# An FFT filter with a soft mixture of experts on one core: another pace for the third chain, two small units two slots later, one copy on ScalarE

## The chip, the cores and the metric

One core of a Trainium2 chip. Its engines are called by the profile's names: PE is TensorE (PEld its weight loads), DVE is VectorE, ACT is ScalarE, POOL is GpSimd, SP is SyncE, which issues nearly all transfers here. The metric is the device time of one execution in microseconds, the median of several runs.

## What is computed

```python
def _attn_ref(x, filt_r, filt_i):            # x: 8 batches, 2496 rows, 256 columns
    X = np.fft.rfft(x, axis=1)
    y = np.fft.irfft(X * (filt_r + 1j * filt_i)[None], n=x.shape[1], axis=1)
...
def _moe_ref(x, phi, w1, w2):                # x: 19968 x 256; 8 experts, 4 slots each
    logits = x @ phi
    d = softmax of logits over the 19968 rows;  slot_input = d.T @ x
    per expert: slot_out = relu(slot_input @ w1) @ w2
    c = softmax of logits over the 32 slots;    return c @ slot_out
```

The filtered sequence is the input of the second part. The first softmax runs over all rows, so it is kept as a running maximum and sum while batch after batch is filtered.

## The kernel before

The length 2496 is split as 39 x 64. Batches 1 to 7 go through these steps, and the steps of neighbouring batches overlap.

- **Units.** A batch's x comes in six pieces, called units 0 to 5 (`PIECE`). `fold_x` (L336, L339) adds and subtracts the two halves of a unit into a tile `eo`, on POOL from batch 2 on; there are two `eo` buffers, so a fold starts when the unit before the last one has been read. `s1_unit` (L357) multiplies a unit on PE into a PSUM tile of a pool with one buffer, ScalarE copies it to `at` (L366), and SP writes `at` to `a_dram`. Unit 0 is half as large as the others.
- **Slots.** Each batch has ten slots. Slot n = 10 b + c loads a tile `ash` from `a_dram`; `x_unit` (L435) multiplies it on PE, DVE makes the two products with the filter (L455, L457) and the two adds that give `yt` (L458, L459; the adds go to POOL for batches 6 and 7). Two slots later `t_unit` (L467) transposes `yt` on PE, ScalarE copies it to `y` (L481), and after every second one `l_unit` (L494) makes logits, copied to `lt` (L505).
- **Which unit in which slot.** `slot_of` gives each unit (b, u) a slot; `split_next` does the fold one slot ahead, and with it the load of a later piece of x.
- **Chains.** When a group of batches is through (0 and 1; 2 and 3; 4 and 5; 6; 7), a chain of dependent work begins (`chain`, L543 on): logits back to the time domain (`ltr`, `v1`, `v`, `lg`), their maximum (`cm`, `cmax`, then `mt`, `mx`, `mb`, `m_run`), the exponentials `d` (L634 on DVE, L635 on ScalarE), a transform of these (`u`, `u2`, `dd`), their sum `z`, and the weighted sum `s` of the rows `y`. Its small tiles use a PSUM pool of two buffers. The chain is a generator: each `yield` is a mark, and after each slot `hop_slot` lets it go some marks further, two (`HOPS`), or for the third chain as many as `PACE` says, slot by slot. So the marks and the pace set which slot work lies between two steps of a chain.
- **The end.** When the third chain's last products are done, the buffers that they free take the experts' weights; the last two chains run in a fixed order (`TAIL`); then come the experts (L1048 to L1077) and the outputs (L1104, L1109), 4-byte floats of 19968 x 256.

Within this, a scheduler places the instructions of each engine in one fixed order, from priorities and its own estimate of times; on the chip each engine works its queue off in that order and waits where an input or a buffer is missing.

Below, an instruction is named as the program names its output: s1_4_5 is unit 5 of batch 4, x_3_4 slot 4 of batch 3, u_0_4 a piece of u of chain 0 (the first chain).

## Time and profile before

| | |
|---|---|
| median of 3 runs | 375.63 us (375.1 to 376.7) |
| the profiled execution | 375.31 us, its span 373.5 us |
| PE busy | 344.2 us (92%) |
| DVE busy | 264.6 us (71%) |
| ACT busy | 175.2 us (47%) |
| POOL busy | 147.0 us (39%) |
| moved by DMA | 104.17 MB, mean 279 GB/s |
| mean granted clock of PE | 0.962 |

Times in the rows count from the start of the span. A row of the timeline has the start, the time from the first to the last of the merged instructions, the engine and line, the tiles written and read, how many instructions there are, and in brackets how long the engine had been idle before and what ended the wait. What ended it is inferred from semaphores: where a wait is for several things, the last by the profile is named. An fp32 matrix product is two instructions in the trace and one in the program.

### The profile page before, as it was taken

What the parts mean: (1) busy time and instruction counts of PE and PEld (TensorE: products, weight loads), DVE (VectorE), ACT (ScalarE), POOL (GpSimd) and SP (SyncE); (2) the same over time, 40 slices, a digit from 0 to 9 for tenths busy, and PEclk for the clock granted to TensorE, in tenths of its full rate; (3) what the DMA queues carried; (4) which work ended last, traced back from release to release, by engine and by line L of the source; (5) the groups of instructions that cost most, each with busy time, mean ns of one, the idle gap of its engine ahead of it and who ended that gap; (6) DMA issues with size and microseconds to landing.
All of it is one profiled execution on the core that took longest, in us unless ns stands there. A gap on an engine that the chain in (4) does not pass through costs nothing. (4 is left out here: it accounts for less than half of the span.)

```text
span 373.5 us, 10516 instructions
## 1 busy us (share of the span) xinstructions
PE 344.2 (92%) x4254; PEld 255.9 (69%) x4254; DVE 264.6 (71%) x522; ACT 175.2 (47%) x354; POOL 147.0 (39%) x177
## 2 busy tenths in 40 slices
PE   8999999899998899999889998899989999999950
PEld 6866766677776577867666775777866635878850
DVE  1586897778998969689996847695675552887540
ACT  3466554454555444545625453533354430766430
POOL 0188655545546213724830754332631302650000
PEclk9999999999999999999999999999999999999555
DMA  8999899799799459979853747642898993699996
GB/s 300 395 396 371 291 329 355 233 342 374 222 350 335 143 163 301 314 235 292 307 185 80 224 138 215 255 142 58 299 355 280 326 272 83 253 411 413 417 419 287
DMA packets 50438, 104.17 MB, mean 279 GB/s; under 512 B 5250, under 2 KB 23810, under 8 KB 48214
## 3 DMA queue, kind: packets, MB, share of 16 engines
q1 hardware_dynamic: 49700, 103.16, 79.4%
q8 instruction: 33, 0.54, 0.6%
q10 hardware_dynamic: 690, 0.35, 0.3%
q14 instruction: 15, 0.12, 0.1%
HBM read 63.37 MB, written 40.12 MB: 277 GB/s over the span
## 5 line engine op out<-in xcount | busy, mean ns | idle before, releaser
L435 PE MATMUL x<-cst_t,ash 128*128 128x128 f32 x640 | 85.7, 276 | 1.7 <-DMA ash<-a_dram 1.7
L455 DVE TENSOR_TENSOR t<-x,ff_t 128x512 f32<-128x512 f32 x80 | 55.1, 689 | 39.0 <-PE x L435 30.5
L336 POOL TENSOR_TENSOR eo<-xt 128x512 f32<-128x512 f32 (+1 forms) x37 | 45.2, 1220 | 94.4 <-issue 89.8
L435 PEld LDWEIGHTS x<-cst_t,ash 128*128 128x128 f32 x640 | 78.1, 192 | 4.0 <-DMA ash<-a_dram 2.6
L366 ACT COPY at<-s 128x1024 f32<-128x1024 f32 (+1 forms) x42 | 39.6, 942 | 47.8 <-PE s L357 27.8
L467 PE MATMUL t<-cst_t,yt 128*128 128x128 f32 x320 | 49.9, 278 | 0.0
L339 POOL TENSOR_TENSOR eo<-xt 128x512 f32<-128x512 f32 (+1 forms) x40 | 48.9, 1221 | 0.0
L481 ACT COPY y<-t 128x512 f32<-128x512 f32 x58 | 33.8, 587 | 30.8 <-PE t L467 30.5
L357 PE MATMUL s<-eo,w1q_t 64*64 64x512 f32 (+1 forms) x336 | 42.8, 579 | 2.7 <-POOL eo L339 2.5
L467 PEld LDWEIGHTS t<-cst_t,yt 128*128 128x128 f32 x320 | 35.9, 141 | 10.2 <-issue 7.1
L457 DVE TENSOR_TENSOR x<-x,ff_t 128x512 f32<-128x512 f32 x60 | 41.7, 696 | 1.3
L1104 PE MATMUL out<-so,st 32*128 32x256 f32 x468 | 35.1, 337 | 2.4 <-ACT ob L1109 1.3
L1104 PEld LDWEIGHTS out<-so,st 32*128 32x128 f32 x468 | 30.7, 222 | 6.1 <-ACT ob L1109 2.9
L494 PEld LDWEIGHTS l<-yt,phi_t 128*32 128x32 f32 x640 | 15.2, 109 | 25.5 <-issue 21.1
L1109 DVE COPY ob<-out 128x512 f32<-128x512 f32 (+1 forms) x40 | 25.0, 669 | 8.5 <-DMA out<-ob 5.8
L458 POOL TENSOR_TENSOR yt<-yt,t 128x256 f32<-128x256 f32 x20 | 15.1, 754 | 35.0 <-DVE yt L457 25.4
L1109 ACT COPY ob<-out 128x512 f32<-128x512 f32 (+1 forms) x40 | 21.7, 582 | 14.8 <-DMA out<-ob 7.8
L458 DVE TENSOR_TENSOR yt<-x,t 128x256 f32<-128x256 f32 x60 | 25.2, 420 | 1.3
L494 PE MATMUL l<-yt,phi_t 128*32 128x128 f32 x640 | 25.7, 278 | 0.0
L459 DVE TENSOR_TENSOR yt<-x,t 128x256 f32<-128x256 f32 x60 | 24.8, 413 | 0.0
L528 PE MATMUL s<-y,dd 128*32 128x256 f32 x232 | 19.2, 381 | 0.3 <-ACT dd L682 0.3
L528 PE MATMUL u<-cst_t,d 117*64 117x60 f32 (+3 forms) x440 | 15.2, 221 | 1.2 <-ACT d L635 1.2
(117 smaller groups left out, 482.1 us busy)
## 6 DMA issues: line engine op xcount, KB each, us to landing
xt<-in_x SPq DMA_DIRECT2D x35, 512.0 KB
ash<-a_dram SPq DMA_DIRECT2D x70, 256.0 KB
out<-ob SPq DMA_DIRECT2D x17, 1024.0 KB
a_dram<-at SPq DMA_DIRECT2D x56, 240.0 KB
w<-in_wx SPq DMA_DIRECT2D x33, 256.0 KB
w<-in_wx SPq DMA_DIRECT2D x6, 512.0 KB
x_t<-in_x SPq DMA_DIRECT2D x5, 512.0 KB
ff_t<-in_ff SPq DMA_DIRECT2D x10, 256.0 KB
```

The costliest lines, as they stand in the source:

```text
L336: ins = (dve if (1, 2) < (b, u) < (2, 0) else eng).tensor_tensor(out=eo[:, 0, 0:n], in0=xs[:, :, 0], in1=xs[:, :, 1], op=ALU.add)
L339: ins = eng.tensor_tensor(out=eo[:, 1, 0:n], in0=xs[:, :, 0], in1=xs[:, :, 1], op=ALU.subtract)
L357: ins = pe.matmul(ps, w1q_t[q, c], eo[q, c, 0:n], start=True, stop=True)
L366: act.copy(at[:, 0:n], both[:, :, 0:n].rearrange("q r u d -> q u r d"))
L435: ins = pe.matmul(ps[:, 2 * k + dh].rearrange("q r c -> q (r c)"), ash[:, k, dh * P : (dh + 1) * P], C("a1" if t0 + k else "b0"), start=Tr ...
L455: dve.tensor_tensor(out=t2, in0=ps[:, :, ::-1, :], in1=fiv, op=ALU.mult)
L457: dve.tensor_tensor(out=part, in0=ps, in1=frv, op=ALU.mult)
L458: add.tensor_tensor(out=yt[:, :, 1, :], in0=part[:, :, 1, :], in1=t2[:, :, 1, :], op=ALU.add)
L467: ins = pe.transpose(pt[:, k, dh, :], yt[:, c % 2, 2 * k + dh].rearrange("q r c -> q (r c)"), ident)
L494: ins = pe.matmul(pl[32 * j : 32 * j + 32, :], phi_t[:, dh, :], yt[:, j // 2, 2 * (j % 2) + dh].rearrange("q r c -> q (r c)"), start=(dh = ...
L1104: nc.tensor.matmul(prs[k][:, mm, :], sts[n][q, hs, c0 : c0 + P], so[q, ho], start=(i == 0), stop=(i == 2))
L1109: copy(ob[:, nm * k : nm * (k + 1), :], prs[k])
```

## The change

Three edits: `PACE` has other numbers and the third chain gets one mark more (`lg8`, between the last piece of lg and `mt`), so that its 14 numbers now add up to 24 instead of 23; unit 0 of batches 5 and 7 has slot 10 b - 14 instead of 10 b - 16, that is 36 instead of 34 and 56 instead of 54; the first of the three copies of u2 in the first two chains is ScalarE's instead of DVE's.

```diff
-PACE = (1, 1, 3, 2, 1, 1, 1, 2, 2, 2, 2, 2, 2, 1)
+PACE = (2, 3, 2, 1, 1, 1, 1, 1, 2, 2, 2, 2, 2, 2)
...
-    return CPB * b - 5 - (2 * (NU - 1 - u) if u else CPB + (b > 2))
+    return CPB * b - 5 - (2 * (NU - 1 - u) if u else CPB + (1, -1)[b in (5, 7)] * (b > 2))
...
-        if late:
+        if g >= NG - 3:
             yield "lg8"
...
-            ended[1] = dve.tensor_copy(u2[:, t0 : t0 + n].rearrange("k t h b e -> k t (h b e)"), pu[:, 0:n])
+            copy = act.copy if t0 == 0 and g < NG - 3 else dve.tensor_copy
+            ended[1] = copy(u2[:, t0 : t0 + n].rearrange("k t h b e -> k t (h b e)"), pu[:, 0:n])
```

What it makes of the order is shown at three places. The number at a name's end is the tile's own; lines after 674 are one higher in the changed kernel. On POOL the folds stand in the order (4,4), (5,0), (4,5), (5,1) before and (4,4), (4,5), (5,0), (5,1) in the change, and in the same way for batches 6 and 7.

First place, PE in slots 34 to 36, with the first chain's u; before:

```order
L357 MATMUL s1_5_0_1721<-eo5_0_1653,w1q_t_72 64x256 x4
L467 MATMUL t_3_3_1736<-cst_t_73,yt_3_2_1633 128x128 x4
L435 MATMUL x_3_5_1743<-cst_t_73,ash3_5_1422 128x128 x4
L528 MATMUL u_0_0_1315<-cst_t_73,d_0_1282 64x60 x12
L357 MATMUL s1_4_5_1753<-eo4_5_1697,w1q_t_72 64x512 x4
L494 MATMUL l_3_1_1760<-yt_3_2_1633,phi_t_74 32x128 x8
L528 MATMUL u_0_0_1315<-cst_t_73,d_0_1282 64x60 x4
L528 MATMUL u_0_4_1336<-cst_t_73,d_0_1282 64x60 x16
L467 MATMUL t_3_4_1779<-cst_t_73,yt_3_4_1715 128x128 x4
L435 MATMUL x_3_6_1786<-cst_t_73,ash3_6_1459 128x128 x4
```

In the change, from slot 35 on:

```order
L467 MATMUL t_3_3_1726<-cst_t_73,yt_3_2_1633 128x128 x4
L435 MATMUL x_3_5_1733<-cst_t_73,ash3_5_1422 128x128 x4
L357 MATMUL s1_4_5_1743<-eo4_5_1692,w1q_t_72 64x512 x4
L494 MATMUL l_3_1_1750<-yt_3_2_1633,phi_t_74 32x128 x8
L528 MATMUL u_0_0_1315<-cst_t_73,d_0_1282 64x60 x16
L528 MATMUL u_0_4_1336<-cst_t_73,d_0_1282 64x60 x16
L467 MATMUL t_3_4_1769<-cst_t_73,yt_3_4_1710 128x128 x4
L435 MATMUL x_3_6_1776<-cst_t_73,ash3_6_1459 128x128 x3
L528 MATMUL u_0_8_1389<-cst_t_73,d_0_1282 64x60 x10
L528 MATMUL u_0_8_1389<-cst_t_73,d_0_1282 64x20 x2
L435 MATMUL x_3_6_1776<-cst_t_73,ash3_6_1459 128x128
L357 MATMUL s1_5_0_1788<-eo5_0_1723,w1q_t_72 64x256 x4
```

The small unit s1_5_0 moves from ahead of t_3_3 to behind x_3_6, and s1_4_5 moves ahead of the chain's u.

DVE at the same place, behind the three subtractions d_0; before:

```order
L455 TENSOR_TENSOR t2_3_4_1714<-x_3_4_1709,ff_t_101 128x512
L457 TENSOR_TENSOR x_3_4_1709<-x_3_4_1709,ff_t_101 128x512
L455 TENSOR_TENSOR t2_3_5_1748<-x_3_5_1743,ff_t_101 128x512
L458 TENSOR_TENSOR yt_3_4_1715<-x_3_4_1709,t2_3_4_1714 128x4x64
L459 TENSOR_TENSOR yt_3_4_1715<-x_3_4_1709,t2_3_4_1714 128x4x64
L457 TENSOR_TENSOR x_3_5_1743<-x_3_5_1743,ff_t_101 128x512
L458 TENSOR_TENSOR yt_3_4_1715<-x_3_5_1743,t2_3_5_1748 128x4x64
L459 TENSOR_TENSOR yt_3_4_1715<-x_3_5_1743,t2_3_5_1748 128x4x64
```

In the change:

```order
L455 TENSOR_TENSOR t2_3_4_1709<-x_3_4_1704,ff_t_101 128x512
L455 TENSOR_TENSOR t2_3_5_1738<-x_3_5_1733,ff_t_101 128x512
L457 TENSOR_TENSOR x_3_4_1704<-x_3_4_1704,ff_t_101 128x512
L457 TENSOR_TENSOR x_3_5_1733<-x_3_5_1733,ff_t_101 128x512
L458 TENSOR_TENSOR yt_3_4_1710<-x_3_4_1704,t2_3_4_1709 128x4x64
L459 TENSOR_TENSOR yt_3_4_1710<-x_3_4_1704,t2_3_4_1709 128x4x64
L458 TENSOR_TENSOR yt_3_4_1710<-x_3_5_1733,t2_3_5_1738 128x4x64
L459 TENSOR_TENSOR yt_3_4_1710<-x_3_5_1733,t2_3_5_1738 128x4x64
```

Both products of x_3_5 move ahead of the adds of the first half of yt_3_4, which t_3_4 reads.

Second place, PE at the transposes u2 of the first chain; before:

```order
L357 MATMUL s1_5_1_1814<-eo5_1_1772,w1q_t_72 64x512 x4
L525 MATMUL u2_0_0_1406<-cst_t_73,u_0_1283 128x128 x4
L525 MATMUL u2_0_4_1449<-cst_t_73,u_0_1283 128x128 x4
L525 MATMUL u2_0_8_1455<-cst_t_73,u_0_1283 128x128 x2
L528 MATMUL dd_0_0_1495<-u2_0_1404,cst_t_73 128x512
L528 MATMUL dd_0_0_1495<-u2_0_1404,cst_t_73 128x64
```

In the change:

```order
L525 MATMUL u2_0_0_1406<-cst_t_73,u_0_1283 128x128 x4
L525 MATMUL u2_0_4_1449<-cst_t_73,u_0_1283 128x128 x4
L357 MATMUL s1_5_1_1814<-eo5_1_1762,w1q_t_72 64x512 x4
L525 MATMUL u2_0_8_1455<-cst_t_73,u_0_1283 128x128 x2
L528 MATMUL dd_0_0_1495<-u2_0_1404,cst_t_73 128x512
L528 MATMUL dd_0_0_1495<-u2_0_1404,cst_t_73 128x64
```

The unit s1_5_1 moves from ahead of the transposes to between the second and the third.

ACT around it; before:

```order
L635 ACTIVATE d_0_1282<-d_0_1282 117x384
L366 COPY at5_0_1726<-s1_5_0_1721 128x512
L481 COPY y_3_3_1741<-t_3_3_1736 128x512
L366 COPY at4_5_1758<-s1_4_5_1753 128x1024
L505 COPY lt_3_1680<-l_3_1_1760 128x128
L663 COPY u_0_1283<-u_0_0_1315 128x10x24 x2
L663 COPY u_0_1283<-u_0_4_1336 128x10x24 x2
L663 COPY u_0_1283<-u_0_8_1389 128x10x18
L663 COPY u_0_1283<-u_0_8_1389 128x10x14
L366 COPY at5_1_1819<-s1_5_1_1814 128x1024
```

In the change:

```order
L481 COPY y_3_3_1731<-t_3_3_1726 128x512
L635 ACTIVATE d_0_1282<-d_0_1282 117x384
L366 COPY at4_5_1748<-s1_4_5_1743 128x1024
L505 COPY lt_3_1675<-l_3_1_1750 128x128
L663 COPY u_0_1283<-u_0_0_1315 128x10x24 x2
L663 COPY u_0_1283<-u_0_4_1336 128x10x24 x2
L663 COPY u_0_1283<-u_0_8_1389 128x10x18
L663 COPY u_0_1283<-u_0_8_1389 128x10x14
L366 COPY at5_0_1793<-s1_5_0_1788 128x512
L675 COPY u2_0_1404<-u2_0_0_1406 128x512
L366 COPY at5_1_1819<-s1_5_1_1814 128x1024
L683 COPY dd_0_1405<-dd_0_0_1495 128x512
```

The copy at5_0 moves behind the copies of u, and the copy of u2_0_0 comes in behind it. On DVE the copy of u2_0_4 moves ahead of the last two adds of yt_3_6. The second chain has the same moves.

Third place, PE in the third chain; before:

```order
L528 MATMUL v1_2_7_2982<-cst_t_73,lsb_2_2886 64x66 x14
L467 MATMUL t_6_2_3017<-cst_t_73,yt_6_2_2916 128x128 x4
L435 MATMUL x_6_4_3024<-cst_t_73,ash6_4_2761 128x128 x4
L528 MATMUL v1_2_14_2998<-cst_t_73,lsb_2_2886 64x66 x12
L467 MATMUL t_6_3_3055<-cst_t_73,yt_6_2_2916 128x128 x4
L435 MATMUL x_6_5_3062<-cst_t_73,ash6_5_2763 128x128 x4
L357 MATMUL s1_7_5_3072<-eo7_5_3012,w1q_t_72 64x512 x4
L494 MATMUL l_6_1_3094<-yt_6_2_2916,phi_t_74 32x128 x8
L525 MATMUL v_2_0_3038<-cst_t_73,v1_2_2965 120x128 x4
L525 MATMUL v_2_4_3044<-cst_t_73,v1_2_2965 120x128 x4
L525 MATMUL v_2_8_3050<-cst_t_73,v1_2_2965 120x128 x3
```

In the change:

```order
L528 MATMUL v1_2_7_2947<-cst_t_73,lsb_2_2886 64x66 x14
L528 MATMUL v1_2_14_2963<-cst_t_73,lsb_2_2886 64x66 x12
L467 MATMUL t_6_2_3037<-cst_t_73,yt_6_2_2925 128x128 x4
L435 MATMUL x_6_4_3044<-cst_t_73,ash6_4_2761 128x128 x4
L525 MATMUL v_2_0_3015<-cst_t_73,v1_2_2930 120x128 x4
L525 MATMUL v_2_4_3021<-cst_t_73,v1_2_2930 120x128 x4
L525 MATMUL v_2_8_3027<-cst_t_73,v1_2_2930 120x128 x3
L467 MATMUL t_6_3_3059<-cst_t_73,yt_6_2_2925 128x128 x4
L435 MATMUL x_6_5_3066<-cst_t_73,ash6_5_2763 128x128 x4
```

v1_2_14 moves ahead of slot 64's t_6_2 and x_6_4, and the three v pieces move up to follow x_6_4. Further on, before:

```order
L528 MATMUL lg_2_4_3128<-v_2_3035,cst_t_73 117x512
L494 MATMUL l_6_2_3160<-yt_6_4_3030,phi_t_74 32x128 x8
L528 MATMUL lg_2_8_3132<-v_2_3035,cst_t_73 117x384
L525 MATMUL mt_2_3137<-cst_t_73,cmax_77 32x117
L467 MATMUL t_6_6_3189<-cst_t_73,yt_6_6_3121 128x128 x4
```

In the change:

```order
L528 MATMUL lg_2_8_3112<-v_2_3012,cst_t_73 117x384
L467 MATMUL t_6_5_3141<-cst_t_73,yt_6_4_3050 128x128 x4
L435 MATMUL x_6_7_3148<-cst_t_73,ash6_7_2824 128x128 x4
L494 MATMUL l_6_2_3160<-yt_6_4_3050,phi_t_74 32x128 x8
L525 MATMUL mt_2_3137<-cst_t_73,cmax_77 32x117
L467 MATMUL t_6_6_3189<-cst_t_73,yt_6_6_3130 128x128 x4
```

A slot's t_6_5 and x_6_7 now stand between lg_2_8 and mt_2; from mt_2 to u_2_0 the order is as before.

DVE there; before:

```order
L455 TENSOR_TENSOR t2_6_4_3029<-x_6_4_3024,ff_t_101 128x512
L457 TENSOR_TENSOR yt_6_4_3030<-x_6_4_3024,ff_t_101 128x512
L455 TENSOR_TENSOR t2_6_5_3067<-x_6_5_3062,ff_t_101 128x512
L457 TENSOR_TENSOR yt_6_4_3030<-x_6_5_3062,ff_t_101 128x512
L590 COPY v_2_3035<-v_2_0_3038 120x512
L590 COPY v_2_3035<-v_2_4_3044 120x512
```

In the change:

```order
L455 TENSOR_TENSOR t2_6_4_3049<-x_6_4_3044,ff_t_101 128x512
L457 TENSOR_TENSOR yt_6_4_3050<-x_6_4_3044,ff_t_101 128x512
L590 COPY v_2_3012<-v_2_0_3015 120x512
L590 COPY v_2_3012<-v_2_4_3021 120x512
L590 COPY v_2_3012<-v_2_8_3027 120x384
L455 TENSOR_TENSOR t2_6_5_3071<-x_6_5_3066,ff_t_101 128x512
L457 TENSOR_TENSOR yt_6_4_3050<-x_6_5_3066,ff_t_101 128x512
```

The copies of v move ahead of the products of x_6_5, behind those of x_6_4.

## Rows read from the trace of the kernel before

**Rows 1.** Busy time by stretches: stretch, length, then each engine's busy time (instructions), clock, DMA.

```profile
112.00:131.00 19.00, 16.57 (x226) 11.15 (x223) 16.59 (x28) 9.47 (x20) 8.53 (x7) 1.00 0.68 235
131.00:180.00 49.00, 49.00 (x598) 36.23 (x590) 40.67 (x83) 24.21 (x43) 20.41 (x18) 1.00 0.83 264
180.00:199.00 19.00, 16.58 (x226) 11.20 (x222) 18.02 (x32) 9.82 (x21) 8.46 (x7) 1.00 0.60 202
...
262.00:318.00 56.00, 53.57 (x802) 35.58 (x801) 29.46 (x75) 20.41 (x55) 15.30 (x30) 1.00 0.81 269
...
330.00:360.00 30.00, 27.92 (x335) 24.93 (x336) 20.15 (x37) 16.37 (x36) 3.77 (x11) 0.75 1.01 416
...
299.00:318.00 19.00, 18.60 (x219) 8.66 (x219) 7.25 (x18) 3.56 (x8) 2.42 (x6) 1.00 0.60 171
```

**Rows 2.** Timeline of PE, first chain: s1_5_0, s1_4_5, t_3_4, u2_0_8, dd_0.

```profile
111.80 0.66 PE L357 MATMUL s<-eo,w1q_t 64*64 64x256 f32 x8
...
116.03 1.09 PE L357 MATMUL s<-eo,w1q_t 64*64 64x512 f32 x8 [1.25 <-POOL eo L339]
...
118.94 0.66 PE L467 MATMUL t<-cst_t,yt 128*128 128x128 f32 x4
...
125.83 0.44 PE L525 MATMUL u<-cst_t,u 128*128 128x128 f32 x2 [0.86 <-DVE u L674]
126.42 2.72 PE L528 MATMUL dd<-u,cst_t 128*128 128x512 f32 x8 [0.16 <-DVE u L674]
```

**Rows 3.** Timeline of ACT, first chain: the copies of s1_5_0 and s1_5_1.

```profile
115.32 0.57 ACT L366 COPY at<-s 128x512 f32<-128x512 f32 x1
...
124.05 1.01 ACT L366 COPY at<-s 128x1024 f32<-128x1024 f32 x1 [2.07 <-issue]
```

**Rows 4.** Timeline of POOL: second half of fold (4,5), both halves of fold (5,1).

```profile
110.88 1.28 POOL L339 TENSOR_TENSOR eo<-xt 128x512 f32<-128x512 f32 x1
112.63 1.82 POOL L336 TENSOR_TENSOR eo<-xt 128x512 f32<-128x512 f32 x1 [0.47 <-POOL eo L339]
114.40 1.59 POOL L339 TENSOR_TENSOR eo<-xt 128x512 f32<-128x512 f32 x1
```

**Rows 5.** Timeline of DVE, first chain: the subtractions d_0, the second half's first add.

```profile
111.45 1.25 DVE L634 TENSOR_TENSOR d<-lg,m_run 117x512 f32<-117x512 f32 x1
...
112.62 0.68 DVE L634 TENSOR_TENSOR d<-lg,m_run 117x512 f32<-117x512 f32 x1
...
113.23 1.63 DVE L634 TENSOR_TENSOR d<-lg,m_run 117x384 f32<-117x384 f32 x1
...
118.09 0.42 DVE L458 TENSOR_TENSOR yt<-x,t 128x256 f32<-128x256 f32 x1
```

**Rows 6.** Timeline of PE, third chain: x_6_4, v_2_0 and v_2_4, v_2_8, mt_2, u_2_0.

```profile
218.94 1.06 PE L435 MATMUL x<-cst_t,ash 128*128 128x128 f32 x8
...
223.85 1.09 PE L525 MATMUL v<-cst_t,v 128*120 128x128 f32 x8
225.29 0.54 PE L525 MATMUL v<-cst_t,v 128*120 128x128 f32 x3 [0.35 <-DVE v L590]
...
232.66 0.26 PE L525 MATMUL mt<-cst_t,cmax 117*32 117x117 f32 x1 [1.04 <-DVE cmax L610]
...
237.87 0.33 PE L528 MATMUL u<-cst_t,d 117*64 117x60 f32 x4 [1.17 <-ACT d L635]
```

**Rows 7.** Timeline of DVE, third chain: second product of x_6_4, copy of v_2_0.

```profile
220.69 0.68 DVE L457 TENSOR_TENSOR yt<-x,ff_t 128x512 f32<-128x512 f32 x1
...
224.54 0.69 DVE L590 COPY v<-v 120x512 f32<-120x512 f32 x1 [0.83 <-PE v L525]
```

**Rows 8.** Timeline of POOL, third chain: one of the adds for yt_6_6.

```profile
229.39 0.73 POOL L459 TENSOR_TENSOR yt<-yt,t 128x256 f32<-128x256 f32 x1
```

**Rows 9.** Timeline of SP and of PE: issue of ash4_0 to ash4_4, and x_4_0.

```profile
123.07 2.24 SPq L308 DMA_DIRECT2D ash<-a_dram  x5
...
139.94 1.06 PE L435 MATMUL x<-cst_t,ash 128*128 128x128 f32 x8
```

## The prediction

> **What bounds the kernel now.** I read the time by stretches first. From 131 to 180 us TensorE is busy in all 49.00 of 49.00 us; at the end the outputs leave at 416 GB/s with the DMA engines' share at 1.01 [rows 1]. So TensorE's queue sets the time up to about 318 us, the writes set it after that, and the writes can only begin earlier if TensorE gets there earlier. A change of this size is therefore worth what it takes out of, or puts into, TensorE's idle time before 318 us, and nothing else. Idle time sits in few places: 2.43 us in 112 to 131 (first chain, slots 34 to 38), 2.42 us in 180 to 199 (second chain, slots 54 to 58), and in the third chain from 217 on [rows 1, 6]. I then listed every gap of TensorE over 0.06 us there, with the work ahead of and behind it, because all three edits act on just these places.
>
> **First edit: the small units of batches 5 and 7.** In slot 35 TensorE waits 1.25 us before s1_4_5 [rows 2]; the second chain's twin waits as long, since its stretch holds the same idle time [rows 1]. The view puts the wait down to POOL, whose operation ends at 115.99. I do not believe it: counted in POOL's order, that operation is the second half of fold (5,1); fold (4,5), which s1_4_5 reads, ended at 112.16 [rows 4]. What ended at 115.89 is ScalarE's copy of s1_5_0 out of PSUM [rows 3], and that pool has one buffer, so s1_4_5 may not start before. The copy was late because it stands in ScalarE's queue behind the third Exp of the chain, whose input VectorE finished only at 114.86 [rows 5]. Why so late? The three subtractions d took 1.25, 0.68 and 1.63 us, the last although it is the smallest [rows 5]; and the folds of (5,1) beside them took 1.82 and 1.59 us against 1.28 us for the one before [rows 4]. They block each other by turns: the first d ends about 0.5 us after a fold ends (112.16 to 112.70), the third likewise (114.45 to 114.86).
>
> In the new order fold (5,1) needs the buffer of fold (4,5), so it starts only after s1_4_5, about 114.5, when the subtractions are over; and fold (5,0), ahead of it, is short and ends near 111.1, before d begins at 111.45. So d should take 0.68 + 0.68 + about 0.5 (384/512 of it, an estimate) and end by 113.3 instead of 114.86: VectorE gains some 1.5 us. The Trainium skill (SBUF — State Buffer, "Who interferes with whom") says that a VectorE operation with both inputs in SBUF and a GpSimd operation that reads SBUF exclude each other for the whole operation, while one with a PSUM input does not; by that rule the fold at its new place, beside products of PSUM tiles, costs nothing, and my sum holds.
>
> With s1_5_0 moved behind it, s1_4_5 needs only s1_4_4's copy, long done: the wait of 1.25 goes. What is late next? TensorE reaches t_3_4 at 118.94 - 1.25 - about 0.6 (s1_5_0 no longer ahead) = 117.1 [rows 2]. t_3_4 needs the adds of the first half of yt. VectorE's order changes here: both products of slot 35's tile now stand ahead of those adds, which end where the second half's adds begin today, 118.09 [rows 5], less the 1.5 gained: 116.6. That is 0.5 us before TensorE comes, so no wait. The term is 1.25 per chain, 2.5 for two; bounds 0.25 (if VectorE gains nothing, t_3_4 waits 1.0) and 1.25. The stores of at5_0 now stand behind those of at4_5 in SP's queue and ahead of the loads ash4_0 to ash4_4; these were issued at 123.07 and are first used at 139.94 [rows 9], and at5_0 is copied near 121, so nothing waits for that.
>
> **Second edit: one copy of u on ScalarE.** After the four transposes of u2_0_4, TensorE waits 0.86 us for a PSUM bank and 0.16 us more before dd [rows 2]: VectorE takes the copy of u2_0_0 only after four other operations. Now ScalarE copies it. A PSUM copy of 128x512 takes 0.57 us there, and ScalarE was idle for 2.07 us just before this place [rows 3]; meanwhile TensorE has u2_0_4 and, moved in between, s1_5_1 (1.09 us, as s1_4_5) to do [rows 2]. So u2_0_8 finds its bank free. dd_0_0 needs VectorE's copy of u2_0_4, which now goes ahead of two adds; from the end of x_3_7 VectorE needs about 1.4 for two products and 0.7 for the copy, TensorE about 2.4 to come to dd_0_0. The term is 0.86 + 0.16 = 1.02 per chain, 2.04 for two; bounds 1.0 (half of it) and 2.04.
>
> **Third edit: the pace of the third chain.** Before, it waits 0.35 (v_2_8), 1.04 (mt_2) and 1.17 (u_2_0) [rows 6]. The new mark lets slot work lie between the last lg and mt: VectorE's cmax is then ready, and 1.04 goes. But the three v groups now directly follow x_6_4. v_2_8 needs the bank of v_2_0, which VectorE copies only after the two products of x_6_4: these end 1.37 us after x_6_4 does (220.00 to 221.37), the copy adds 0.69 [rows 6, 7], and TensorE has two v groups, 1.09 us, in that time [rows 6]. So v_2_8 waits 2.06 - 1.09 = about 1.0 in place of 0.35. Next, t_6_6 and t_6_7 need two POOL adds of 0.73 us each [rows 8] behind products that VectorE does later than before; I estimate 0.35 us of wait in all (bounds 0 and 0.7). From mb to u_2_0 the order is the same, so that wait stays near 1.17. Out: 0.35 + 1.04. In: 1.0 + 0.35. Term: 0, bounds -0.5 and +1.4.
>
> **Sum.** 2.5 + 2.0 + 0 = 4.5 us. Against the profiled execution's 375.31 us that is 370.8; the median of the runs is 375.63, 0.3 above it, so I predict 371.1, faster by 1.2%. A measurement of this kernel can tell about 0.5%, or 1.9 us, from no change.
>
> **Rivals.**
> (a) No lock: the long subtractions are long of themselves, VectorE gains nothing, and t_3_4 and t_5_4 wait about 1.0. Then the first edit gives 0.25 per chain, and the whole 0.5 + 2.0 = 2.5: 373.1. If half the second term goes too, 374.1. For it: a profile shows durations, not locks. Against: the two engines' long operations end in each other's gaps. If the skill's rule named above were wrong, this would be the case. 0.16.
> (b) The third chain is better than I count: VectorE copies v_2 in time, and the wait at mt is gone without a substitute: 1.4 more, 369.7; with the wait at u_2_0 gone as well, 368.6. For it: VectorE had free time there before. Against: its order puts the products first. 0.17.
> (c) The weights become the bound. From 262 to 318 the DMA share is 0.81 [rows 1]; if their transfers do not begin earlier, TensorE waits for them and gives all back: 375.6. Against: most go into buffers that the third chain's last products free, so they move along, and TensorE's whole idle time in that stretch is 2.4 us [rows 1]. 0.11.
> (d) Slower: TensorE's clock. The granted clock is 1.00 (2.4 GHz) through every stretch up to 318 and 0.75 on average in 330 to 360 [rows 1], so it does fall to 1.2 GHz while TensorE still works. If with other waits it fell before the experts' stage, the 18.6 us of work from 299 to 318 would take twice as long: 371.1 + 18.6 = 389.7; a fall from about 4.5 us of work before 318 on is the point where the gain is gone. Against: waits of 1.25 us did not lower it here, and the change leaves fewer of them. 0.03.
>
> **How the numbers follow.** My forecast has the remaining 0.53. Faster by over 0.5% (below 373.75): 0.53 + 0.17 + most of (a), 0.10 = 0.80. Within 0.5%: the rest of (a) and (c), 0.17. Slower: 0.03. The range, 368.9 to 373.8, runs from the better end of (b) into (a), and leaves out (c), (d) and the edges of (a) and (b), about 0.2.
>
> **What would show it.** Right: no wait at s1_4_5 and s1_6_5; d_0 and d_1 in three even operations of 0.5 to 0.7 us; t_3_4 without a wait; no wait at u2_0_8; TensorE's idle time about 0.2 us in each of the two stretches; in the third chain a new wait of about 1 us at v_2_8, none at mt_2 and about 1 us left at u_2_0; the first output some 4.5 us earlier and the output stage as long as before. Wrong: d still locked with a fold, or TensorE waiting at t_3_4, or gaps after 262 that were not there.

## The result and the profile after

The changed kernel takes 369.77 us (median of 6 runs, 369.25 to 370.29) against 375.57 us (375.10 to 376.70) for the kernel before on the same chip: a ratio of 0.9842, 95% interval 0.9827 to 0.9858, or 5.8 us less. The prediction was 371.1 us, 4.5 less, and its range held the result. Its single terms did not hold: the first and the third were too small, the second too large, and the experiments show how.

First the stretches of the kernel after, the view of [rows 1] (stretch, length, busy time and instructions of PE, PEld, DVE, ACT, POOL, then clock, DMA share, GB/s):

```profile
112.00:131.00 19.00, 18.84 (x279) 12.84 (x281) 15.77 (x30) 11.25 (x22) 7.55 (x6) 1.00 0.75 254
131.00:180.00 49.00, 49.00 (x568) 36.34 (x562) 41.37 (x84) 25.55 (x47) 20.41 (x19) 1.00 0.84 271
180.00:199.00 19.00, 18.52 (x284) 12.77 (x277) 14.39 (x29) 9.70 (x20) 7.53 (x6) 1.00 0.62 204
262.00:318.00 56.00, 53.50 (x803) 35.38 (x803) 31.34 (x81) 22.63 (x61) 16.15 (x34) 1.00 0.75 256
...
330.00:360.00 30.00, 26.37 (x274) 24.77 (x270) 17.07 (x30) 14.30 (x29) 0.92 (x4) 0.50 1.01 416
```

TensorE's idle time fell from 2.43 to 0.16 us in the first stretch and from 2.42 to 0.48 in the third (0.32 of it a new wait at t_5_4); at the end the outputs leave at 416 GB/s as before. There the granted clock is now 0.50 (1.2 GHz) from 330 us on. That costs nothing, since the DMA engines' share is 1.01 either way and the last outputs come 5.5 us earlier.

The first chain on PE, the view of [rows 2]: s1_4_5, t_3_4, u2_0_8 and dd_0 without a wait, and z_0.

```profile
113.40 1.09 PE L357 MATMUL s<-eo,w1q_t 64*64 64x512 f32 x8
...
117.01 0.66 PE L467 MATMUL t<-cst_t,yt 128*128 128x128 f32 x4
...
123.60 0.44 PE L525 MATMUL u<-cst_t,u 128*128 128x128 f32 x2
123.93 2.72 PE L528 MATMUL dd<-u,cst_t 128*128 128x512 f32 x8
126.81 0.30 PE L528 MATMUL z<-cst_t,dd 128*32 128x1 f32 x16 [0.16 <-ACT dd L683]
```

DVE's three subtractions d_0, which took 1.25, 0.68 and 1.63 us [rows 5], are now one merged row:

```profile
111.72 1.76 DVE L634 TENSOR_TENSOR d<-lg,m_run 117x512 f32<-117x512 f32 x3
```

and POOL's fold (5,1), 1.82 and 1.59 us before [rows 4], starts after them and runs at full pace:

```profile
114.66 1.28 POOL L336 TENSOR_TENSOR eo<-xt 128x512 f32<-128x512 f32 x1 [3.32 <-issue]
115.90 1.28 POOL L339 TENSOR_TENSOR eo<-xt 128x512 f32<-128x512 f32 x1
```

The third chain on PE, the view of [rows 6]: v_2_8, mt_2 (no wait), t_6_6, u_2_0.

```profile
218.36 0.55 PE L525 MATMUL v<-cst_t,v 128*120 128x128 f32 x3 [1.16 <-DVE v L590]
...
227.55 0.28 PE L525 MATMUL mt<-cst_t,cmax 117*32 117x117 f32 x1
228.09 0.66 PE L467 MATMUL t<-cst_t,yt 128*128 128x128 f32 x4 [0.26 <-POOL yt L459]
...
233.20 1.15 PE L528 MATMUL u<-cst_t,d 117*64 117x60 f32 x32 [1.09 <-ACT d L635]
```

To see where the 5.6 us of span went I compared the start of the same product in both traces at five places. From t_3_2 to t_3_6 (first chain) the kernel after takes 21.65 us against 24.18, in the second chain's twin 22.01 against 24.18, from t_6_1 to t_7_3 46.31 against 47.45; before the first chain it is 0.3 us later, in waits for the ash loads, which differ from execution to execution (t_3_2 starts between 109.6 and 112.0 us in the traces of this document). That is 2.53 + 2.17 + 1.14 - 0.3 = 5.5. Of the first two, 2.27 and 1.94 are idle time; of the third only 2.73 - 2.53 = 0.20 is. So some 1.4 us came from TensorE being busy for less time with the same number of products, a term that the prediction does not have: 0.26 and 0.23 us in the first two chains, 0.94 in the third.

The part in the first two chains can be placed. In a row of 128x128 products each lasts 0.27 us in the trace and the next starts 0.11 us after it, so ahead of a wait 0.16 us counts as busy that would otherwise lie beside the next product. An estimate from this: three waits less (at s1_4_5, u2_0_8 and dd_0) are worth 0.48 us beyond their idle time, and from t_3_2 to z_0 TensorE is busy for 16.07 us against 16.56. About half of it is lost again behind z: there the l unit among the products of s now starts behind the third of a set of four, where it stood between two sets before, and from z_0 to t_3_6 the kernel after takes 5.43 us against 5.19, in the second chain likewise.

### The profile page after: what moved, and what is told of

It reads as the page before. It is cut to its first block, busy times and chain, and to the rows that moved or that the text cites. A ratio compares the mean times of both kernels' runs of the same rounds, so it can differ in the third digit from the quotient of the medians.

```text
span 367.9 us, 10511 instructions
## 1 busy us (share of the span) xinstructions
PE 344.9 (94%) x4254; PEld 259.4 (71%) x4254; DVE 258.4 (70%) x520; ACT 177.4 (48%) x356; POOL 144.4 (39%) x177
## 4 chain that ended last, share of the span: by engine, by line
PE 76%; DVE 8%; DMA 5%; ACT 3%; POOL 2%; issue 2%; SPq 1%; DVEq 0%; ACTq 0%; POOLq 0%
PE x L435 16%; PE s L357 9%; PE t L467 8%; PE out L1105 7%; PE s L528 5%; PE l L494 4%; DMA ash<-a_dram 4%; PE u L528 3%; PE s L408 3%; PE dd L528 3%; PE lg L528 3%; PE v L528 2%; PE h L1049 2%; PE o L1067 2%; DVE ob L1110 2%
## 5 line engine op out<-in xcount | busy, mean ns | idle before, releaser
L336 POOL TENSOR_TENSOR eo<-xt 128x512 f32<-128x512 f32 (+1 forms) x37 | 44.0, 1189 | 91.8 <-issue 85.8
L366 ACT COPY at<-s 128x1024 f32<-128x1024 f32 (+1 forms) x42 | 39.6, 944 | 45.0 <-PE s L357 26.6
L339 POOL TENSOR_TENSOR eo<-xt 128x512 f32<-128x512 f32 (+1 forms) x40 | 48.3, 1208 | 0.0
L1105 PE MATMUL out<-so,st 32*128 32x256 f32 x468 | 36.2, 368 | 1.1 <-DVE ob L1110 0.8
L1105 PEld LDWEIGHTS out<-so,st 32*128 32x128 f32 x468 | 32.8, 254 | 3.8 <-DVE ob L1110 1.7
L494 PE MATMUL l<-yt,phi_t 128*32 128x128 f32 x640 | 26.5, 279 | 0.0
L481 ACT COPY yb<-t 128x512 f32<-128x512 f32 x20 | 11.7, 586 | 9.8 <-PE t L467 9.8
```

What stands on the lines that cost most here:

```text
L336: ins = (dve if (1, 2) < (b, u) < (2, 0) else eng).tensor_tensor(out=eo[:, 0, 0:n], in0=xs[:, :, 0], in1=xs[:, :, 1], op=ALU.add)
L339: ins = eng.tensor_tensor(out=eo[:, 1, 0:n], in0=xs[:, :, 0], in1=xs[:, :, 1], op=ALU.subtract)
L481: act.copy(y, pt.rearrange("k p h d -> k p (h d)"))
L494: ins = pe.matmul(pl[32 * j : 32 * j + 32, :], phi_t[:, dh, :], yt[:, j // 2, 2 * (j % 2) + dh].rearrange("q r c -> q (r c)"), start=(dh = ...
L1105: nc.tensor.matmul(prs[k][:, mm, :], sts[n][q, hs, c0 : c0 + P], so[q, ho], start=(i == 0), stop=(i == 2))
```

## Experiments

All times are medians beside the kernel before on the same chip (375.7 to 375.9 us); gains are the ratio's distance from 1 times 375.6.

### The three edits one by one

Each edit alone, and the first two together. The first, e1_slots, keeps from the change only this line:

```diff
-    return CPB * b - 5 - (2 * (NU - 1 - u) if u else CPB + (b > 2))
+    return CPB * b - 5 - (2 * (NU - 1 - u) if u else CPB + (1, -1)[b in (5, 7)] * (b > 2))
```

> The change's first edit alone (new slots for the small units of batches 5 and 7); copies of u stay on VectorE, the third chain keeps its old pace. By the prediction's terms: the wait of 1.25 us at s1_4_5 and its twin goes, the waits at u2_0_8 and dd stay, so 2.5 us less than before, 373.1 us. By the theory formed from the changed kernel's trace (the terms overlap): moving s1_5_1 behind the two transposes of u already gives VectorE time to empty the bank, so the 0.86 at u2_0_8 goes with this edit too, and only a wait of about 0.67 us before dd is left in place of 0.16 (VectorE makes both copies, 0.68 each, behind a product). That is 1.25 + 0.35 per chain, 3.2 in all, and about 0.3 less for fewer switches of tile shape: 372.1 us. Rival, POOL's fold was what s1_4_5 waited for: the wait stays, 375.6 us.

Measured: 370.70 us, ratio 0.9875 (0.9849 to 0.9900), 4.7 us less. Most of the gain comes with this edit. PE in the first chain, u2_0_8 and dd_0:

```profile
122.98 0.44 PE L525 MATMUL u<-cst_t,u 128*128 128x128 f32 x2
123.78 2.72 PE L528 MATMUL dd<-u,cst_t 128*128 128x512 f32 x8 [0.36 <-DVE u L674]
```

and DVE beside it, the copies of u2_0_0 and u2_0_4 around the second product of x_3_7:

```profile
121.86 0.68 DVE L674 COPY u<-u 128x512 f32<-128x512 f32 x1
122.45 0.69 DVE L457 TENSOR_TENSOR x<-x,ff_t 128x512 f32<-128x512 f32 x1
123.05 0.68 DVE L674 COPY u<-u 128x512 f32<-128x512 f32 x1
```

The wait of 0.86 at u2_0_8 is gone with the copy still on VectorE. With the small unit moved, s1_5_1 (1.09 us) stands behind the two transposes, the scheduler puts VectorE's first copy ahead of a product, and the bank is empty in time. What is left for the second edit is 0.36 us before dd (0.37 in the second chain). The overlap theory is right in kind; it put that rest at 0.67, and the whole at 3.5 instead of 4.7.

e2_copy keeps only the copy on ScalarE:

```diff
-            ended[1] = dve.tensor_copy(u2[:, t0 : t0 + n].rearrange("k t h b e -> k t (h b e)"), pu[:, 0:n])
+            copy = act.copy if t0 == 0 and g < NG - 3 else dve.tensor_copy
+            ended[1] = copy(u2[:, t0 : t0 + n].rearrange("k t h b e -> k t (h b e)"), pu[:, 0:n])
```

> The second edit alone: ScalarE makes the first copy of u in the first two chains, slots and pace as before. By the prediction's terms 1.02 us per chain goes, 2.04 in all: 373.6 us. By the overlap theory: without the new slots s1_5_1 still stands ahead of the transposes, so ScalarE's queue has the copy of s1_5_1 (1.01 us, ending at 125.06 in the trace of before) ahead of the copy of u, which then ends at 125.63 instead of VectorE's 125.77; u2_0_8 still waits about 0.7 us, dd comes about 0.35 earlier per chain: 0.7 us in all, 374.9 us. Rival: no gain at all, 375.6 us.

Measured: 374.97 us, ratio 0.9985 (0.9969 to 1.0001), 0.6 us less; the interval just includes no change, so the waits have to tell. u2_0_8 on PE:

```profile
125.60 0.44 PE L525 MATMUL u<-cst_t,u 128*128 128x128 f32 x2 [0.64 <-ACT u L675]
```

ACT, the copy of s1_5_1 and the copy of u2_0_0 behind it:

```profile
124.05 1.01 ACT L366 COPY at<-s 128x1024 f32<-128x1024 f32 x1 [2.08 <-issue]
124.95 0.59 ACT L675 COPY u<-u 128x512 f32<-128x512 f32 x1
```

The copy ends at 125.54, where VectorE's ended at 125.77. u2_0_8 waits 0.64 us in place of 0.86 and dd_0 not at all, in both chains: TensorE's idle time falls by 0.39 us per chain, where the edit was booked at 1.02. Behind the first edit it takes 0.36 per chain, about as much as alone.

e3_pace keeps the new numbers of PACE and the added mark lg8:

```diff
-PACE = (1, 1, 3, 2, 1, 1, 1, 2, 2, 2, 2, 2, 2, 1)
+PACE = (2, 3, 2, 1, 1, 1, 1, 1, 2, 2, 2, 2, 2, 2)
...
-        if late:
+        if g >= NG - 3:
```

> The third edit alone: new pace of the third chain with its added mark, slots and copies as before. By the prediction's term (waits alone: out 0.35 and 1.04, in about 1.0 and 0.35) the time stays 375.6 us, within 0.5. By the switching theory the waits cancel as forecast, but the products of one tile shape now lie together (the inverse transform's products behind each other, the last two l units where the row groups go on in turn), which takes 0.9 us off TensorE's busy time in that stretch without any wait: 374.5 us, with TensorE's idle time in 217 to 245 us about as before. Rival, the gain seen there came from the first two edits having shifted the weights' and units' arrival: 375.6 us or above.

Measured: 374.70 us, ratio 0.9971 (0.9954 to 0.9989), 1.1 us less. The waits are those of the kernel after (1.16, 0.26, 1.09). The stretch from t_6_1 to t_7_3, kernel before:

```profile
213.64:261.09 47.45, 44.72 (x621) 34.09 (x620) 32.36 (x55) 20.85 (x43) 19.80 (x26) 1.00 0.53 166
```

and in e3_pace:

```profile
214.39:260.74 46.35, 43.82 (x621) 34.66 (x620) 31.85 (x55) 20.71 (x43) 19.66 (x27) 1.00 0.53 168
```

The same 621 matrix instructions, 0.90 us less busy. One place shows how: PE's products of v1 of the fourth chain and of dd_2, kernel before, in three pieces:

```profile
249.05 0.53 PE L528 MATMUL v<-cst_t,lsb 128*32 128x66 f32 x10
249.51 1.12 PE L528 MATMUL dd<-u,cst_t 128*128 128x512 f32 x2
250.57 0.42 PE L528 MATMUL v<-cst_t,lsb 128*32 128x66 f32 x6
250.92 0.70 PE L528 MATMUL dd<-u,cst_t 128*128 128x256 f32 x2
251.55 0.54 PE L528 MATMUL v<-cst_t,lsb 128*32 128x66 f32 x12
```

and in the kernel after, all 28 in one piece:

```profile
243.78 1.00 PE L528 MATMUL v<-cst_t,lsb 128*32 128x66 f32 x28
```

A row's time reaches to the end of its last product, beside which the next row has begun; counted to the start of what follows, the three pieces take 0.46 + 0.35 + 0.47 = 1.28 us against 0.93. Counted along PE's order, the array passes 30 times from tiles of one width (128, 64 or 32 output rows) to another in that stretch before, and 24 times in e3_pace and after. The 0.9 us had been read off the changed kernel's trace before this run; what the run adds is that it belongs to the third edit alone. That it is the switches is argued from their price, which is measured below: six at about 0.1 us are 0.6 of the 0.9. Some 0.16 more fits one wait less; the rest is not assigned.

e4_slots_copy has the first two edits:

> First and second edit together, the third chain with its old pace. By the prediction's terms 2.5 + 2.0 = 4.5 us: 371.1 us; the overlap theory gives the same waits, and 0.5 us more for fewer switches of tile shape, so 370.8 us, and the step from this kernel to the changed one is what the third edit brings alone, about 1.1 us. If the first edit alone is at 372.1 and the second alone at 374.9, their sum is 4.2 against some 4.8 together: the second is worth more behind the first. Rival, edits independent: 3.2 or 2.5 plus 0.7 or 2.0 exactly.

Measured: 370.47 us, ratio 0.9869 (0.9847 to 0.9891), 4.9 us less. Alone the edits gave 4.7 and 0.6, and with these intervals a sum of 5.3 cannot be told from 4.9. The traces can tell: from t_3_2 to t_3_6 TensorE's idle time falls by 1.91 us with the first edit, by 0.39 with the second and by 2.27 with both, so the waits add up. That the second is worth more behind the first, as expected, is not seen; the rival, independent edits, holds for the waits, with other sizes than the forecast's. The step from here to the whole change is the third edit once more, 1.0 us by the ratios and 1.1 from t_6_1 to t_7_3 in the traces.

### What s1_4_5 waited for

at_first is the kernel before with ScalarE's order turned round in one place: the third Exp of each of the first two chains behind the copy of s1_5_0 or s1_7_0.

```diff
-        act.copy(at[:, 0:n], both[:, :, 0:n].rearrange("q r u d -> q u r d"))
+        ins = act.copy(at[:, 0:n], both[:, :, 0:n].rearrange("q r u d -> q u r d"))
+        if (b, u) in ((5, 0), (7, 0)):
+            not_before(third_exp[(b - 5) // 2], ins)
...
-            act.activation(d[:, x0:x1], d[:, x0:x1], AF.Exp)
+            ins = act.activation(d[:, x0:x1], d[:, x0:x1], AF.Exp)
+            if a0 == 8:
+                third_exp[g] = ins
```

> The kernel before with one thing turned round on ScalarE: in the first two chains the copy of s1_5_0 (and s1_7_0) out of PSUM goes ahead of the third Exp instead of behind it; slots, copies of u and pace as before, POOL's folds untouched. If s1_4_5 waited for that copy (its PSUM pool has one buffer), the copy ends near 114.6 instead of 115.89 and the wait of 1.25 us goes in both chains with nothing late behind it (t_3_4's operands were ready at 117.44, TensorE comes at 117.7): 2.5 us less than before, 373.1 us. If the profile's releaser is right (POOL's operation that ends at 115.99), the wait stays 1.25: 375.6 us. The three subtractions and the folds stay as long as before in either case (1.25, 0.68, 1.63 and 1.82, 1.59).

Measured: 378.12 us, ratio 1.0064 (1.0043 to 1.0086), 2.4 us more. PE, first chain: s1_4_5, then u2_0_8.

```profile
114.88 1.09 PE L357 MATMUL s<-eo,w1q_t 64*64 64x512 f32 x8
...
125.49 0.44 PE L528 MATMUL u<-cst_t,u 128*128 128x128 f32 x2 [1.40 <-DVE u L679]
```

POOL, the second half of fold (5,1):

```profile
114.68 1.60 POOL L339 TENSOR_TENSOR eo<-xt 128x512 f32<-128x512 f32 x1
```

On the question asked the answer is clear: s1_4_5 starts without a wait at 114.88 while the POOL operation that the profile names as its releaser still runs until 116.28. It waited for the PSUM buffer. But the forecast of the time failed, since I looked at the first chain's nearest consumer alone. Three things gave the 2.5 us back, and more: a wait in the second chain, a longer one at u2_0_8, and the clock. In the second chain t_5_4 waits:

```profile
189.10 0.63 PE L470 MATMUL t<-cst_t,yt 128*128 128x128 f32 x4 [2.11 <-DVE alc L703]
```

VectorE has two operations on al ahead of its operands there, 128x32 with both inputs in SBUF, which take 0.18 us without POOL beside them; in at_first:

```profile
183.97 1.25 DVE L699 TENSOR_TENSOR al<-m_run,m_run 128x32 f32<-128x32 f32 x1
...
186.47 1.22 DVE L701 TENSOR_TENSOR al<-al,cst_t 128x32 f32<-128x32 f32 x1
```

and the first of them in the kernel before:

```profile
182.65 1.25 DVE L694 TENSOR_TENSOR al<-m_run,m_run 128x32 f32<-128x32 f32 x1
```

So the first was long in the kernel before too, beside the second half of a fold, and t_5_4's operands were ready at 186.58, only 0.22 us before TensorE came at 186.80; a TensorE that comes 1.24 us earlier waits 1.0. The other 1.04 us is the second operation, 0.18 us in the kernel before: with s1_6_5, the twin of s1_4_5, earlier, its fold buffer came free earlier, and POOL's next fold fell on this operation. The wait at u2_0_8 grew from 0.86 to 1.40 in both chains. And behind the first of these waits the clock fell, as the windows of this run show:

```profile
122.00:126.00 4.00, 2.53 (x19) 1.24 (x18) 3.97 (x10) 1.01 (x1) 2.50 (x2) 1.00 0.60 174
126.00:130.60 4.60, 4.33 (x8) 1.96 (x8) 3.57 (x6) 1.17 (x3) 0.00 (x0) 0.63 0.37 134
130.60:134.00 3.40, 3.35 (x76) 2.10 (x80) 2.45 (x5) 2.61 (x6) 0.00 (x0) 1.00 0.28 63
```

A mean of 0.63 says that most of the 4.60 us ran at 1.2 GHz; from dd_0 to z_0 it took 4.57 us against 2.88 in both kernels compared here. Behind the same two waits in the second chain (1.40 and 0.16 us) it stayed at 1.00. The sum: -2 x 1.24 + 2 x 0.54 + 2.11 + 1.69 = 2.4, which is what was measured.

### The lock

lock is the changed kernel with extra work for POOL beside d:

```diff
+        if g < NG - 3:
+            junk = wk.tile([KR, 16, SLOTS], mybir.dt.bfloat16, tag="junk", name=f"junk_{g}", bufs=1)
+            for _ in range(2):
+                pool_e.tensor_tensor(out=junk, in0=lgf[:, 0:16], in1=mbc.broadcast_to([KR, 16, SLOTS]), op=ALU.subtract)
         dispatch(0)
```

> The changed kernel with two more POOL subtractions per chain in the first two chains (117x512, both inputs in SBUF, their result is used by nothing), which become ready together with VectorE's subtractions d. If the two engines shut each other out during operations on SBUF, d no longer takes 0.68, 0.68 and 0.55 but at least 1.3 us more in all, VectorE's products and adds come as much later, and TensorE waits some 0.8 to 2.1 us before t_3_4 and t_5_4: 371.4 to 374 us against 369.8 for the changed kernel. Rival, no lock, long subtractions were long of themselves: d stays at 1.9 us in all, time 369.8 us. The later fold (5,1) moves by less than its slack in either case.

Measured: 376.92 us (373.31 to 377.91 in the nine executions that the ratio counts), ratio 1.0013 (0.9987 to 1.0040); the profiled execution is the fastest, 373.31. In it DVE's d and POOL's two operations:

```profile
110.75 3.93 DVE L634 TENSOR_TENSOR d<-lg,m_run 117x512 f32<-117x512 f32 x3
```

```profile
110.79 3.48 POOL L640 TENSOR_TENSOR junk<-lg,m_run 117x512 bf16<-117x512 f32 x2 [0.43 <-DVE m_run L624]
```

and t_3_4 on PE:

```profile
117.89 0.63 PE L467 MATMUL t<-cst_t,yt 128*128 128x128 f32 x4 [1.78 <-DVE yt L459]
```

d takes 3.93 in place of 1.76 with nothing but POOL's work added: its first operation, begun ahead of POOL's, 0.69 us, the other two 1.77 and 1.64, each ending about 0.5 us after one of POOL's. t_3_4 waits 1.78 and t_5_4 3.06, more than the forecast's 2.1, since al is locked there too (1.26 us). This is the forecast mechanism, the "no lock" rival falls. The traced execution lies in the forecast's range, 371.4 to 374; the median lies 3 us above it, in executions of which there is no trace. In the traced one the clock stayed at 1.00 behind both waits. The others' mean granted clock is on record: 0.938 to 0.942 in four of the eight, where the kernel before has 0.949 to 0.966 on that chip. That points to a clock that fell earlier in them, as in at_first, but does not show it.

### The price of a switch

Two runs on TensorE's order alone, beside the changed kernel on the same chip (after_again).

> The changed kernel unchanged, on the same chip as the next three, so that differences of about a microsecond can be read: 0.984 of the kernel before, TensorE's idle time about 1.2 us at v_2_8 and 1.1 us at u_2_0 as in its first trace.

Measured: 369.80 us, ratio 0.9844 (0.9820 to 0.9869), waits of 1.16 and 1.10 us.

mix alters seven slots:

```diff
+MIXED = tuple((5, u) for u in (2, 3, 4, 5)) + tuple((6, u) for u in (2, 3, 4))
...
-                if floor is None:
+                if (b, u) in MIXED:
+                    if (c, r) == (0, 0):
+                        not_before(ins, x_parts[3])
+                    elif (c, r) == (1, 0):
+                        not_before(ins, x_parts[1])
+                    elif (c, r) == (1, 1):
+                        not_before(ins, first)
+                        not_before(x_parts[2], ins)
+                    else:
+                        not_before(ins, first)
+                    first = ins
+                elif floor is None:
...
+                x_parts[2 * k + dh] = ins
```

> The changed kernel with TensorE's order altered in seven slots of the stretch where it has no idle time (131 to 199 us; slots with s1_5_2 to s1_5_5 and s1_6_2 to s1_6_4): two products of x, two of s1, two of x, two of s1, in place of four and four. Same products, same operands, no wait in the old order there. By the switching theory each switch between tiles of 128 and of 64 output rows costs about 0.1 us (0.205 from start to start after the last product of x where s1 follows, 0.109 where another tile of 128 rows does; 0.52 after a product of s1 of 0.43), and each slot has two more of them: 0.2 us per slot, 1.3 us in all, 371.1 us against 369.8 for the changed kernel, without a new wait. Rival, a switch of tile shape is free and what the third edit gained came from elsewhere: same time as the changed kernel.

Measured: 378.78 us, ratio 1.0081 (1.0059 to 1.0103), 9 us above the changed kernel instead of 1.3, and no new wait. One slot on PE in mix:

```profile
134.61 0.61 PE L448 MATMUL x<-cst_t,ash 128*128 128x128 f32 x4
135.15 1.07 PE L358 MATMUL s<-eo,w1q_t 64*64 64x512 f32 x4
136.15 0.71 PE L448 MATMUL x<-cst_t,ash 128*128 128x128 f32 x4
136.79 1.08 PE L358 MATMUL s<-eo,w1q_t 64*64 64x512 f32 x4
```

and in the changed kernel:

```profile
135.51 1.06 PE L435 MATMUL x<-cst_t,ash 128*128 128x128 f32 x8
136.49 1.09 PE L357 MATMUL s<-eo,w1q_t 64*64 64x512 f32 x8
```

The switches cost what was forecast: from start to start, a product of x before another of x takes 0.112 us and before one of s1 0.205, which is 0.09 more, and the last product of s1 before x gives another 0.10, so 0.2 us per slot. What I had missed is larger. The four products of s1 lie on the four quarters of the array side by side (they start within 0.02 us of each other), and two of them take 1.07 us, as long as all four (1.09); split in pairs by a product that needs the whole array, a unit costs 2.15. Seven times 1.0 + 0.2 is 8.4, which is the longer busy time from z_0 to t_5_4 (63.92 us against 55.60 in after_again); the rest of the 9 us is not placed. The Trainium skill (TensorEngine Tiling (Array Packing), "Key Properties") says that a change of the tiling mode drains TensorE; the rows agree, at 0.1 us a change.

l_rows changes the order within a unit:

```diff
-            for dh in range(2):
-                for j in range(4):
+            for j in range(4):
+                for dh in range(2):
```

> The changed kernel with the eight products of each l unit (32 output rows each, four groups of rows) in another order: both products of a group of rows behind each other, where they went round the four groups before. By the theory that products on different groups of rows run beside each other, and one on the same group waits for the one before, a unit takes longer than the 0.64 us of now, at least 0.1 us more for each of 40 units, so 374 us or above, with TensorE busier and not more idle. Rival, the order of the groups is free: 0.64 us, 369.8 us.

Measured: 370.77 us in one run; the 640 instructions of l are busy for 26.6 us against 26.5. The rival holds, as far as one run can tell: which of the four groups a product goes to next cost these products nothing.

### A version that beats both

v_act changes one copy of the changed kernel:

```diff
-            dve.tensor_copy(v[:, s0 : s0 + n, :], pv[:, 0:n])
+            (act.copy if g == NG - 3 and s0 == 0 else dve.tensor_copy)(v[:, s0 : s0 + n, :], pv[:, 0:n])
```

> The changed kernel with the copy of v_2_0 in the third chain on ScalarE, which is idle from 216.1 on there. The prediction said the wait at v_2_8 is for VectorE's copy behind two products: then the copy ends near 217.45 instead of 218.30, the wait falls from 1.16 to about 0.3 us, and nothing behind it is late (the other two copies of v are made 0.7 us earlier on VectorE): 0.85 us less than the changed kernel, 368.9 us. Rival, the wait only moves on to the next meeting with VectorE (t_6_6 or mt): 369.8 us.

Measured: 368.90 us, ratio 0.9814 (0.9791 to 0.9837); v_2_8 waits 0.29 in place of 1.16, as forecast, and from t_6_1 to t_7_3 the trace has 45.43 us in place of 46.31.

v_dfirst adds an order of issue: the second product of x_6_8 behind the first subtraction of d_2, and u_2_4 behind t_6_8.

```diff
+        if (b, c) == (PA, CPB - 2):
+            not_before(ins, first_d[NG - 3])
...
+        if (b, c) == (PA, CPB - 2):
+            not_before(u4_first[0], ins)
```

> As the run with the copy of v_2_0 on ScalarE, and in the third chain VectorE makes the first subtraction of d ahead of the second product of x_6_8, so that POOL's two adds (0.73 and, beside d, 1.18 us in the changed kernel's trace) start after it. If the wait of 1.09 at u_2_0 comes from d being shut out by these adds, the first d takes 0.68, the first Exp comes about 1.3 us earlier and the wait at u_2_0 goes; the adds then meet the second d, and t_6_8 waits 0.25 to 1.3 us: between 0 and 0.85 less than the run before, 368.1 to 368.9 us. Rival, d is slow for another reason: first d as long as now, 368.9 us or above.

Measured: 368.50 us, ratio 0.9813 (0.9789 to 0.9837): the wait at u_2_0 is gone, and t_6_8 has one of 0.98, the poor end of what was forecast. That is no gain over v_act: the ratios agree, and from t_6_1 to t_7_3 the trace has 45.67 us against 45.43. POOL's adds beside d:

```profile
230.25 1.02 POOL L462 TENSOR_TENSOR yt<-yt,t 128x256 f32<-128x256 f32 x1 [2.17 <-DVE yt L459]
231.24 1.04 POOL L463 TENSOR_TENSOR yt<-yt,t 128x256 f32<-128x256 f32 x1
```

v_best moves the other two subtractions behind the products of x_6_9, which read PSUM, and u_2_4 behind x_7_0:

```diff
...
+        if (b, c) == (PA, CPB - 1):
+            not_before(second_d[0], ins)
...
+        if (b, c) == (PA + 1, 0):
+            not_before(u4_first[0], ins)
```

> The changed kernel with the copy of v_2_0 on ScalarE, the first subtraction of d ahead of the second product of x_6_8, the other two behind the products of x_6_9 (these read PSUM, so POOL's adds beside them should not be shut out), and the second part of u behind x_7_0 on TensorE. In the run before this one the wait at u_2_0 had gone, but POOL's adds met the second and third subtraction (1.02 and 1.04 us in place of 0.73) and t_6_8 waited 0.98. If that was the lock, the adds take 0.73 again, t_6_8 waits about 0.25, u_2_4 not at all: 0.7 us less than that run and 1.6 less than the changed kernel, 368.1 us. Rival, the wait only moves on once more: 368.9 us.

Measured: 368.29 us (366.69 to 368.51), ratio 0.9798 (0.9774 to 0.9822), 1.5 us below the changed kernel on the same chip (0.9820 to 0.9869, so the intervals just touch). From t_6_1 to t_7_3 the trace has 44.68 us in place of 46.31, 1.6 less as forecast. The same two adds on POOL:

```profile
231.55 0.73 POOL L467 TENSOR_TENSOR yt<-yt,t 128x256 f32<-128x256 f32 x1 [2.18 <-DVE yt L462]
232.24 0.73 POOL L468 TENSOR_TENSOR yt<-yt,t 128x256 f32<-128x256 f32 x1
```

and t_6_8 on PE:

```profile
233.02 0.66 PE L476 MATMUL t<-cst_t,yt 128*128 128x128 f32 x4 [0.38 <-POOL yt L468]
```

Beside VectorE operations on PSUM the adds take 0.73 again, beside d they took 1.02. The two subtractions that moved now meet the adds of x_6_9, which take 1.18 and 1.04 us; TensorE does not wait for these. Of 2.5 us of waits in the third chain 0.9 is left.

## Why the prediction was right, and where not

**What bounds the kernel.** Right: every microsecond taken out of TensorE's queue before 318 us came out at the end, 5.6 of span with the output stage unchanged. Wrong: that a change is worth what it takes out of TensorE's idle time "and nothing else". Some 1.4 us of the gain is busy time. The rivals on the weights (c) and on the clock in this change (d) did not come true; at_first shows that the clock can fall before the experts' stage, there for most of 4.6 us and at a price of 1.7.

**First edit, the mechanism.** Right in the steps that were named: the wait was for ScalarE's copy (at_first), d and the fold no longer lock each other (rows above, lock), t_3_4 comes without a wait. t_5_4 waits 0.32 us, which the prediction did not say: the second chain has the operations on al as well, one of them beside the fold.

**First and second edit, the sizes.** This is the step that failed: "The term is 0.86 + 0.16 = 1.02 per chain, 2.04 for two" was booked to the copy on ScalarE, although the same paragraph has s1_5_1 "moved in between", which is the first edit's doing. Measured: 4.7 us for the first alone (2.5 in the prediction, bounds 0.5 and 2.5) and 0.6 for the second alone (2.04, bounds 1.0 and 2.04): both lie outside their bounds. In waits per chain: the first edit takes 1.91 us, its own 1.25 and 0.66 of what was booked to the second, and the second 0.39. Together that is 2.27, the sum of the two terms, 1.25 and 1.02: the total held because each wait was counted once, under the wrong name. In the second chain 0.32 of it comes back at t_5_4.

**Third edit.** The waits came as worked out: 1.16 at v_2_8 (1.0), none at mt_2, 0.26 at t_6_6 (0.35), 1.09 at u_2_0 (1.17); the stretch's idle time fell by 0.20. The term was put at 0 and measured at 1.1, inside its bounds, because only idle time was counted: TensorE was busy for 0.9 us less with the same instructions. Six switches of width less account for some 0.6 of that at the price that mix shows; the rest is argued or open. This 0.9 and the 0.5 us of busy time in the first two chains make up most of the difference between 4.5 and 5.8. That the result lay in the range is in part luck: its better end, 368.9, stood for rival (b), a wait less, and not for busy time.

**The rivals.** (a) fell with the lock run. (b) gave the right time, 369.7, for the wrong reason: VectorE did not copy v_2 in time. v_act shows what its mechanism is worth, 0.9 us more.

## What to carry to other kernels

Price a wait by the whole order and not by the edit that is nearest to it: here two thirds of the wait that one edit was priced for went with another, and only a run of each alone tells which one does it. When matrix products of different widths are reordered, count how often the array changes its width and whether sets that run side by side stay whole, since this moves time with no wait to be seen. Where VectorE and POOL both work from SBUF, place one beside the other's PSUM operations; releasing a wait early can pull the next operation into the lock.

## What was unexpected of the hardware

- Two products on quarters of the array take as long as four (1.07 and 1.09 us), and a change of width between products of 128x128 and of 64x64 costs about 0.1 us; in mix 8.3 us of busy time were added in seven slots without any new wait.
- An operation of 128x32 elements on VectorE took 1.25 us instead of 0.18 beside a fold of 1.58 us on POOL: what a locked operation cost here went by the other engine's length and not by its own.
- The granted clock fell to a mean of 0.63 behind waits of 1.40 and 0.16 us in the first chain of at_first. It stayed at 1.00 behind the same two waits in the second chain, and behind waits of 1.78 and 3.06 in the lock run: the length of a single wait did not decide it here, and what did stays open.
